# Seven products instead of eight for two token blocks of the second weight chunk, in an attention + experts + MLP kernel

## The chip, the core and the metric

One core of a Trainium2 chip runs the kernel. The metric is the device time of one execution in microseconds (us); the median of several executions counts. PE is the matrix engine, DVE the vector engine, ACT the scalar engine, POOL the GpSimd engine, SP the engine whose queue issues the loads.

## The reference

Sliding-window attention with sink tokens gives x (1536 tokens by 512). A mixture of eight experts follows, its gate balanced by eight rounds of row and column scaling, and then a two-layer MLP:

```python
P = np.exp(x @ w_gate - max)
for _ in range(8):
    P /= P.sum(1) + 1e-09;  P /= P.sum(0) + 1e-09;  P *= N / E
for e in range(8):
    out += P[:, e:e + 1] * (np.maximum(x @ w1[e], 0) @ w2[e])      # F = 1024
g = np.maximum(out @ w_in, 0) ** 2                                 # 2048 wide
return g @ w_out
```

Everything is float32.

## The kernel before, in words

**Chunks and blocks.** The weights are worked through in 20 chunks `c`, each 512 columns of a first matrix and the 512 matching rows of a second; 16 belong to the experts, 4 to the MLP. Chunk 0 runs as filler inside the attention (`phase_a`, its last groups at the start of `phase_b`), chunks 1 to 19 in `phase_b`. The tokens are three blocks `t` of 512. A float32 operand is held as a high and a low part, and one product of two operands is three matmuls. A split (`pair_split`, L480) writes the high part on ACT and then the low part on POOL.

**First product.** `plain(c, t, f)` makes 128 columns `f` of one block with 12 matmuls into one PSUM bank. From chunk 2 on `fast(c, half, 0)` (L793) makes two column groups of the blocks 0 and 1 together, as a two-by-two block product with seven multiplications instead of eight. Its seven steps are p1, p6, p5, p2, p7, p3, p4, of six matmuls each, each with an evacuation e1 to e4, e6 and so on behind it. It needs four sums of parts of x (`T1` to `T4`, made by `sums(0)` on DVE and split; T1 overwrites the part B12 of x) and four sums of weight parts (`unit_sums` on POOL, then split by `units(.., 3, ..)`). The third block has sums of its own (`sums(1)`). Step p1 fills a bank, e1 has ACT copy it to the scratch tile `x0` as `s`, and p2 goes on adding into the same bank, so p2 waits for that copy:

```python
def e1():
    v["s"] = self.scratch2("xs" if q else "x0", w)
    nc.scalar.activation(out=v["s"], in_=v["a"], func=AF.Copy)
...
def p2():
    mul("a", "A12", "B21")
```

The scratch tiles `x0`, `x1`, `x2` and `u` have one buffer each; who writes one waits until everything that read its last content is done. `sums` and the steps of `fast` share them.

**Second product.** `second(c, t)` (L899) is four groups of 12 matmuls; DVE adds each to `acc`.

**Order.** Every engine takes its instructions in the order in which the program issues them. `phase_b` builds a list `seq` of groups for a chunk and a `plan` of further steps behind each group; the position of a group in `seq` is called its position here. In chunk 1 the first run is a plain group and the three left groups of chunk 0. Then all three blocks go through `plain` (blocks 1, 0, then 2) with the second products between. `part_w2` splits the second matrix, `sums(0)` is made at positions 0 to 12 for chunk 2, `sums(1)` at positions 15 to 21, the weight sums of chunk 2 at positions 7 to 10.

**The gate** (`gate`, L946) is a generator with 14 steps: three logit steps of eight matmuls, the maximum, and eight rounds. In each round DVE makes the column sums `cs`, PE adds them over the partitions by one small matmul, and DVE scales P. One step is issued behind each group whose number is in `GATE_AT`. The weight `wgz` of the gate and the matrix `ones` are made at the start of `phase_b`. P is first needed in the second product of chunk 2.

**Loads.** `load_list` orders the 512 KB loads of the weights into three raw buffers; a load is issued when the one three places before it is used up.

Of the kernel before, what the change touches and what calls it, by code (L numbers as in the profile page):

```python
# [39 lines left out]
CONV_AT = (0, 1, 2, 3, 8, 9, 10, 11, 12, 13, 14, 15)  # L40
GATE_AT = (0, 1, 2, 3, 5, 7, 9, 11, 13, 16, 19, 22, 25, 30)
W2_AT = (2, 5, 8, 11)
# [6 lines left out]
class Kernel:  # L49
# [30 lines left out]
    def masks_begin(self):  # L80
# [19 lines left out]
        self.ident = c.tile([128, 128], F32, name="ident")  # L100
        make_identity(nc, self.ident)
        a = self.att
        self.junk = a.tile([128, 1], F32, name="junk")
# [332 lines left out]
    def load_list(self, c0):  # L436

        loads, k = [(c0, which, half) for which in range(2) for half in range(2)], 0
        for c in range(c0, NC):
            wide = [(j, 2, 0) for j in range(k, min(k + CONV, 8 * NC2)) if c >= 2]  # L440
            k += len(wide)
            n = c + 1
            loads += wide[0:1]
            if n < NC:
                if self.is_fast(n):
                    loads += [(n, 3, 0), (n, 3, 1)]
                loads += wide[1:2] + [(n, 0, 0)] + wide[2:3] + [(n, 0, 1), (n, 1, 0), (n, 1, 1)]
            else:
                assert len(wide) < 2
        return loads  # L450
# [219 lines left out]

    def sums(self, q):

        nc = self.nc
        T = [
            self.tp.tile([128, 3, 2, NB >> q], F32R, tag=f"T{q}{t}", name=f"T{q}{t}")
            for t in "hl"
        ]
        self.T[q] = T

# [9 lines left out]
        def put(name, kc, x):  # L689
            hi, lo = self.operand(name, q)  # L690
            self.pair_split(hi[:, kc], lo[:, kc], x)

        for kc in range(2):
            x = tt("x0", f32("B22", 0, kc), f32("B12", 0, kc), ALU.subtract)
# [347 lines left out]
    def run(self):  # L1042
# [18 lines left out]
        if True:  # L1061
            with tc.manual_schedule():
                first = ExitStack()
                self.wp = self.pool(first, "wp0")
                self.hp0 = self.pool(first, "hp0")
                with ExitStack() as actx:
                    self.wraw = self.pool(actx, "wraw0")
# [125 lines left out]
    def phase_a(self, gen):  # L1193
# [17 lines left out]
        for n in (HP - 1, HP):  # L1211
            self.att_load_qk(n)
        fill = self.filler(gen)
        at = next(fill)
        for u in range(U + 2):
# [57 lines left out]
            if u == 20:  # L1273
                self.general_flag()
        return fill

    def phase_b(self, c0, first, fill):
# [20 lines left out]
        self.next_loads()  # L1298
        self.wgz = self.xp_.tile([128, KD, 128], F32R, tag="x0", name="wgz")
        wgr = self.xp_.tile([128, KD, E], F32, tag="x2", name="wgr")  # L1300
        nc.gpsimd.memset(self.wgz.bitcast(F32), 0.0)
        self.ones = self.xp_.tile([128, 128], F32, tag="x1", name="ones")
        nc.gpsimd.memset(self.ones, 1.0)
        nc.sync.dma_start(out=wgr, in_=self.wg)
        todo = [partial(self.units, c0, half, 0, k) for half in range(2) for k in range(2)]
        for _ in fill:
# [7 lines left out]
        hz = self.wgz[:, :, 0:E]  # L1314
        nc.scalar.activation(out=hz, in_=wgr, func=AF.Copy)
        nc.vector.tensor_tensor(
            out=self.wgz[:, :, E : 2 * E], in0=wgr, in1=hz.bitcast(F32), op=ALU.subtract
        )
        gate = self.gate()
        groups = itertools.count()  # L1320

        def run(seq, plan):

            for k, g in enumerate(seq):
                g()
                for step in plan.get(k, ()):
                    step()
                if next(groups) in GATE_AT:
                    next(gate, None)
# [5 lines left out]
        for c in range(c0, NC):  # L1335
# [8 lines left out]
            if not low:  # L1344
                run([self.plain(c, 1, 0), *rest], {})
                low = first.close() or True
                self.w2p = self.pool(left, "w2" + n)
                self.tp = self.pool(left, "T" + n)
                self.cp, self.T = self.pool(left, "c" + n), {}
                seq = [self.plain(c, t, f) for t in (1, 0) for f in range(KD)][1:]  # L1350
# [10 lines left out]
            if self.is_fast(c):  # L1361
                (a, b, *e), (f, g, *i) = (self.fast(c, half, 1) for half in range(2))
# [13 lines left out]
            if c == NC1 - 1:  # L1376
# [3 lines left out]
                )  # L1380
                wide = lambda k: m + k if k < 8 else m + 2 * k - 8
            else:
                seq += self.second(c, 0) + self.second(c, 2)
                wide = lambda k: m + k
            if c in (FAST - 1, FAST2 - 1):
                t = self.sums(0)
                for k in range(13):
                    put(k if c < FAST else min(2 * k, k + 5), next, t, None)
# [111 lines left out]
```

## Time and profile before

| | |
|---|---|
| median of 3 runs | 1379.15 us (1378.8 to 1379.48) |
| profiled execution | 1379.64 us, of which the span from first to last instruction is 1377.8 us |
| busy in the span | PE 1363.2, DVE 955.4, POOL 501.3, ACT 453.1 us |
| granted clock of PE | 0.999 of full speed |
| attention ends on PE / chunk 1 starts / chunk 2 starts | 150.87 / 163.67 / 247.35 us |

The kernel is one chain of matmuls: PE is busy 99% of the span. The times of the last row are read from the start of the span. A bar on PE in the trace is longer than the distance to the next, since matmuls overlap; costs are taken from start to start.

### The profile page before, as it was taken

How to read it: one execution, taken by the hardware profiler on the slowest of the kernel's cores; microseconds unless marked ns; L12 is line 12 of the kernel's file. 1: busy time of each engine (PE TensorE's matmuls, PEld its weight loads, DVE VectorE, ACT ScalarE, POOL GpSimd, SP SyncE). 2: the span in 40 equal slices, each digit the busy share in tenths (PEclk: the TensorE clock that was granted, in tenths of full speed). 3: DMA queues.
4: the chain of work that ended last, by engine and by line, in shares of the span. 5: the costliest groups of instructions: out<-in, count | busy, mean ns of one | idle time of the engine just before them, and what ended most of it. 6: DMA issues, size and time to landing. Idle time of an engine off the chain costs nothing.

```text
span 1377.8 us, 18905 instructions
## 1 busy us (share of the span) xinstructions
PE 1363.2 (99%) x7105; PEld 1141.7 (83%) x7105; DVE 955.4 (69%) x1884; ACT 453.1 (33%) x1007; POOL 501.3 (36%) x442
## 2 busy tenths in 40 slices
PE   8999999999999999999999999999999999999998
PEld 5677888888888888888888888888888888888887
DVE  8777369887777777777777768765454568866564
ACT  6776322322232222222232222222232243433331
POOL 4322136524343434424343434423343036543210
PEclk9999999999999999999999999999999999999999
DMA  5222200132313232232313232230102010111101
GB/s 203 81 90 73 78 31 31 62 94 73 124 54 109 79 96 85 92 107 67 118 54 122 70 95 82 92 107 32 61 32 77 16 62 16 62 55 54 46 24 72
DMA packets 61147, 102.53 MB, mean 74 GB/s; under 512 B 3957, under 2 KB 43253, under 8 KB 60789
## 3 DMA queue, kind: packets, MB, share of 16 engines
q1 hardware_dynamic: 61040, 101.22, 23.2%
q8 instruction: 58, 0.95, 0.3%
q14 instruction: 45, 0.36, 0.1%
q10 hardware_dynamic: 4, 0.00, 0.0%
HBM read 89.67 MB, written 11.53 MB: 73 GB/s over the span
## 4 chain that ended last, share of the span: by engine, by line
PE 79%; DVE 1%; ACT 0%; issue 0%; DVEq 0%; ACTq 0%
PE mm L913 42%; PE mm L762 36%; PE mm L930 0%; ACT tx L733 0%; DVE acc L653 0%; DVE tx L734 0%; ACT hh L745 0%; DVE tx L822 0%; DVE hl L746 0%; DVE acc L649 0%; DVE mm L734 0%; DVE raw L578 0%; ACT tx L836 0%; DVE tu L822 0%; DVE raw L565 0%
## 5 line engine op out<-in xcount | busy, mean ns | idle before, releaser
L913 PE MATMUL mm<-w2h,hh 128*128 128x512 f32 (+1 forms) x916 | 357.0, 390 | 0.0
L913 PE MATMUL mm<-w2l,hh 128*128 128x512 f32 (+1 forms) x916 | 355.9, 388 | 0.0
L913 PE MATMUL mm<-w2h,hl 128*128 128x512 f32 (+1 forms) x916 | 355.6, 388 | 0.0
L482 POOL TENSOR_TENSOR w2l<-raw,w2h 128x512 fp32r<-128x512 f32 x76 | 118.5, 1559 | 365.7 <-ACT w2h L481 363.7
L653 DVE SCALAR_TENSOR_TENSOR acc<-mm,P,acc 128x512 f32<-128x512 f32 x168 | 125.7, 748 | 135.6 <-PE mm L913 134.4
L913 PEld LDWEIGHTS mm<-w2h,hl 128*128 128x128 f32 x916 | 172.0, 188 | 35.8
L913 PEld LDWEIGHTS mm<-w2h,hh 128*128 128x128 f32 x916 | 172.1, 188 | 34.6
L913 PEld LDWEIGHTS mm<-w2l,hh 128*128 128x128 f32 x916 | 172.1, 188 | 34.3
L525 POOL TENSOR_TENSOR raw<-raw 128x256 f32<-128x256 f32 x136 | 125.1, 923 | 7.9
L482 POOL TENSOR_TENSOR s0l<-raw,s0h 128x512 fp32r<-128x512 f32 (+1 forms) x36 | 45.5, 1264 | 198.6 <-ACT s0h L481 198.6
L730 ACT ACTIVATE hh<-tx 128x512 fp32r<-128x512 f32 (+1 forms) x112 | 58.8, 525 | 130.0 <-DVE tx L822 129.5
L822 DVE TENSOR_TENSOR tx<-mm,tu 128x512 f32<-128x512 f32 (+1 forms) x136 | 75.6, 556 | 20.9 <-PE mm L762 16.6
L822 DVE TENSOR_TENSOR tx<-mm,tx 128x512 f32<-128x512 f32 (+1 forms) x68 | 37.9, 557 | 57.8 <-PE mm L762 56.5
L740 DVE SCALAR_TENSOR_TENSOR hl<-tx,hh 128x512 fp32r<-128x512 f32 (+1 forms) x112 | 70.1, 626 | 9.7 <-ACT hh L730 9.6
L836 ACT ACTIVATE tx<-mm 128x512 f32<-128x512 f32 x34 | 20.3, 598 | 154.9 <-PE mm L762 153.0
L646 DVE TENSOR_TENSOR acc<-mm,acc 128x512 f32<-128x512 f32 (+1 forms) x49 | 33.2, 677 | 48.2 <-PE mm L913 47.9
L730 ACT ACTIVATE hh<-mm 128x512 fp32r<-128x512 f32 (+1 forms) x68 | 34.0, 501 | 99.2 <-PE mm L762 99.2
L836 ACT ACTIVATE txs<-mm 128x256 f32<-128x256 f32 x34 | 13.0, 381 | 151.3 <-PE mm L762 151.3
L482 POOL TENSOR_TENSOR a0l<-raw,a0h 128x512 fp32r<-128x512 f32 (+1 forms) x38 | 43.0, 1148 | 51.5 <-ACT a0h L481 47.5
L762 PE MATMUL mm<-xl,a1h 128*128 128x512 f32 (+1 forms) x172 | 60.3, 350 | 0.2 <-ACT tx L836 0.2
L762 PE MATMUL mm<-xl,a0h 128*128 128x512 f32 (+1 forms) x172 | 59.8, 348 | 0.0
L762 PE MATMUL mm<-xh,a0h 128*128 128x512 f32 (+1 forms) x172 | 59.8, 347 | 0.0
(262 smaller groups left out, 3149.5 us busy)
## 6 DMA issues: line engine op xcount, KB each, us to landing
raw<-w SPq DMA_DIRECT2D x110, 512.0 KB, 3.7
raw<-win SPq DMA_DIRECT2D x16, 512.0 KB, 4.0
w<-m SPq DMA_DIRECT2D x32, 256.0 KB, 4.6
raw<-wout SPq DMA_DIRECT2D x16, 512.0 KB, 4.0
raw<-qkv SPq DMA_DIRECT2D x8, 624.0 KB, 5.0
raw<-qkv SPq DMA_DIRECT2D x7, 464.0 KB, 3.9
out<-acc SPq DMA_DIRECT2D x11, 256.0 KB, 2.0
wraw<-w SPq DMA_DIRECT2D x2, 1024.0 KB, 6.7
```

The lines of the kernel that those rows point to most:

```text
L482: self.nc.gpsimd.tensor_tensor(out=lo, in0=src, in1=hi.bitcast(F32), op=ALU.subtract)
L525: self.nc.gpsimd.tensor_tensor(out=o, in0=x, in1=y, op=op)
L646: nc.vector.tensor_tensor(out=a, in0=ps, in1=a, op=ALU.add)
L653: nc.vector.scalar_tensor_tensor(out=a, in0=ps, scalar=self.P[:, ti, e : e + 1], in1=a, op0=ALU.mult, op1=ALU.add)
L730: nc.scalar.activation(out=hh, in_=src, func=AF.Relu)
L740: nc.vector.scalar_tensor_tensor(out=hl, in0=src, scalar=0.0, in1=hh.bitcast(F32), op0=ALU.max, op1=ALU.subtract,)
L762: self.nc.tensor.matmul(out=ps, lhsT=w[:, kc], rhs=x[:, kc], start=start and k == 0, stop=(k == n - 1), skip_group_check=True,)
L822: nc.vector.tensor_tensor(out=v[name], in0=v[a], in1=v[b], op=ALU.add)
L836: nc.scalar.activation(out=v["s"], in_=v["a"], func=AF.Copy)
L913: self.nc.tensor.matmul(out=ps[:, d], lhsT=x[:, f, s], rhs=w[:, f, d], start=(n == 0), stop=(n == 11),)
```

## The change

Chunk 1 is reordered. The third block goes first and stays plain, its second product follows, then blocks 0 and 1 go through `fast` together, and their second products end the chunk. So the first product of chunk 1 has 84 matmuls in two blocks where it had 96.

For that the sums of x must be there earlier. T1 is made in the end of the attention's filler, behind the three logit steps of the gate (T1 overwrites a part of x that they read). T2, T3 and T4 are made at positions 3 to 8 of chunk 1, under the second product of the third block and the first steps of `fast`. The weight sums of chunk 1 are new work: two more loads of 512 KB, eight POOL additions and four splits. The gate's weight is loaded and split inside the attention (units 20 and 25), `ones` is made at the kernel's start. Ten steps of the gate are left for the groups numbered 12 to 41.

```diff
-GATE_AT = (0, 1, 2, 3, 5, 7, 9, 11, 13, 16, 19, 22, 25, 30)
+GATE_AT = (
+    (0, 1, 2, 3, 5, 7, 9, 11, 13, 16, 19, 22, 25, 30),
+    (12, 15, 18, 21, 24, 27, 30, 33, 37, 41),
+)
...
+        self.ones = c.tile([128, 128], F32, name="ones")
+        nc.gpsimd.memset(self.ones, 1.0)
...
+        if c0:
+            loads[2:2] = [(c0, 3, 0)]
+            loads.append((c0, 3, 1))
...
+    def sums(self, q, t1_first=False):
...
+        if t1_first:
+            for kc in range(2):
+                x = tt("x0", f32("B12", 0, kc), f32("B11", 0, kc), ALU.subtract)
+                tt(x, x, f32("B12", 1, kc), ALU.add)
+                tt(x, x, f32("B11", 1, kc), ALU.subtract)
+                put("T1", kc, x)
+                yield
+            self.T_tiles(q)
+            t2 = []
+            for kc in range(2):
+                x = tt(("u", "x1")[kc], f32("B22", 0, kc), f32("B12", 0, kc), ALU.subtract)
+                tt(x, x, f32("B22", 1, kc), ALU.add)
+                tt(x, x, f32("B12", 1, kc), ALU.subtract)
+                put("T2", kc, x)
+                t2.append(x)
+                yield
+            for kc in range(2):
+                x = tt("x0", t2[kc], f32("B11", 0, kc), ALU.subtract)
+                tt(x, x, f32("B11", 1, kc), ALU.subtract)
+                put("T3", kc, x)
+                yield
+            for kc in range(2):
+                x = tt("x2", f32("B21", 0, kc), t2[kc], ALU.subtract)
+                tt(x, x, f32("B21", 1, kc), ALU.add)
+                put("T4", kc, x)
+                yield
+            return
...
+            if u in (20, 25):
+                gw.pop(0)()
...
+    def gate_weights(self, pool, tags):
...
+        def load():
+            nc.gpsimd.memset(self.wgz.bitcast(F32), 0.0)
+            nc.sync.dma_start(out=wgr, in_=self.wg)
+
+        def split():
+            nc.scalar.activation(out=hz, in_=wgr, func=AF.Copy)
+            nc.gpsimd.tensor_tensor(
+                out=self.wgz[:, :, E : 2 * E], in0=wgr, in1=hz.bitcast(F32), op=ALU.subtract
+            )
...
+            early = [partial(next, gate)] * 3 + [partial(next, t0)] * 2
+            early += [partial(self.unit_sums, c0, 0, k) for k in range(2)]
+            early.append(partial(next, gate))
+        for at in fill:
             if self.done:
                 self.evac()
                 if todo:
                     todo.pop(0)()
+                if early and (at == NT - QW or len(early) > 5):
+                    early.pop(0)()
         self.evac()
-        for step in todo:
+        for step in todo + early:
             step()
...
-                run([self.plain(c, 1, 0), *rest], {})
+                run([self.plain(c, 1 + c0, 0), *rest], {})
...
+            mixed = c == c0 == 1
             for k in range(4):
-                put(W2_AT[k] if self.is_fast(c) else k, self.part_w2, c, k)
+                if mixed:
+                    self.part_w2(c, k)
...
+            if mixed:
+                m += 18
+                put(2, self.finish)
+                seq += self.second(c, 2) + self.fast(c, 0, 0) + self.fast(c, 1, 0)
+                seq += self.second(c, 1)
+                for k in range(2):
+                    put(2 + 2 * k, self.units, c, 0, 3, k)
+                    put(6 + k, self.unit_sums, c, 1, k)
+                    put(8 + k, self.units, c, 1, 3, k)
...
+            elif mixed:
+                seq += self.second(c, 0)
+                wide = lambda k: m - 8 + k
...
+                t = t0 if mixed else self.sums(0)
+                for k in range(7 if mixed else 13):
+                    put(k + 3 if mixed else min(2 * k, k + 5) if c >= FAST else k, next, t, None)
                 t = self.sums(1)
                 for k in range(13):
-                    put(m + 8 + k // 2, next, t, None)
+                    put(m + (k // 2 if mixed else 8 + k // 2), next, t, None)
```

In the new chunk 1 the positions are: 0 to 2 plain groups of block 2, 3 to 6 its second product, 7 to 13 the steps p1, p6, p5, p2, p7, p3, p4 of the first half, 14 to 20 those of the second half, 21 to 24 the second product of block 1, 25 to 28 that of block 0. Group number is position plus 4.

## Rows read from the trace of the kernel before

**Rows 1.** The page: the span, and the busy time of each engine.
```profile
span 1377.8 us, 18905 instructions
...
PE 1363.2 (99%) x7105; PEld 1141.7 (83%) x7105; DVE 955.4 (69%) x1884; ACT 453.1 (33%) x1007; POOL 501.3 (36%) x442
```

**Rows 2.** Busy time by stretch: from and to, length, then each engine, clock, DMA.
```profile
150.87:163.67 12.80, 12.80 (x69) 12.02 (x68) 4.21 (x7) 4.35 (x10) 6.16 (x10) 1.00 0.53 169
163.67:181.70 18.03, 18.03 (x86) 14.14 (x85) 2.28 (x5) 2.97 (x6) 0.00 (x0) 1.00 0.08 28
...
204.50:226.90 22.40, 22.18 (x102) 18.11 (x101) 21.05 (x36) 6.26 (x11) 15.27 (x15) 1.00 0.00 1
226.90:247.35 20.45, 20.45 (x95) 16.99 (x93) 18.62 (x39) 4.80 (x11) 11.02 (x12) 1.00 0.24 78
```

**Rows 3.** PE in order of time, chunk 2: first matmuls of p1, p6 and p2.
```profile
247.35 0.39 PE L762 MATMUL mm<-xl,a0h 128*128 128x512 f32 x1
...
248.71 0.39 PE L762 MATMUL mm<-T0l,s0h 128*128 128x512 f32 x1
...
251.43 0.39 PE L762 MATMUL mm<-xl,a0h 128*128 128x512 f32 x1
```

**Rows 4.** PE in order of time: the two waits in chunks 1 and 2.
```profile
210.04 0.39 PE L913 MATMUL mm<-w2h,hl 128*128 128x512 f32 x1
210.64 0.39 PE L1001 MATMUL mm<-cs,ones 128*128 128x8 f32 x2 [0.21 <-DVE cs L995]
...
280.99 0.28 PE L762 MATMUL mm<-xh,a0l 128*128 128x256 f32 x1
281.86 0.39 PE L762 MATMUL mm<-xl,s0h 128*128 128x256 f32 x1 [0.59 <-DVE tx L822]
```

**Rows 5.** DVE in order of time: sums of x, evacuations, one round of the gate.
```profile
186.03 1.79 DVE L683 TENSOR_TENSOR tx<-tx,tu 128x512 f32<-128x512 f32 x1
...
190.46 1.78 DVE L683 TENSOR_TENSOR tu<-xl 128x512 f32<-128x512 f32 x1
192.17 0.68 DVE L740 SCALAR_TENSOR_TENSOR hl<-mm,hh 128x512 fp32r<-128x512 f32 x1
...
198.44 0.68 DVE L683 TENSOR_TENSOR tu<-xl 128x512 f32<-128x512 f32 x1
199.04 0.68 DVE L740 SCALAR_TENSOR_TENSOR hl<-mm,hh 128x512 fp32r<-128x512 f32 x1
...
204.78 0.69 DVE L646 TENSOR_TENSOR acc<-mm,acc 128x512 f32<-128x512 f32 x1
...
230.17 0.20 DVE L1005 RECIPROCAL cs<-mm 128x8 f32<-128x8 f32 x1
...
231.67 0.35 DVE L995 TENSOR_REDUCE cs<-P 128x8 f32<-128x104 f32 x1
```

**Rows 6.** POOL in order of time: attention, start of the weights, low parts, weight sums.
```profile
72.16 2.32 POOL L205 TENSOR_TENSOR qkl<-raw,qkh 128x640 fp32r<-128x640 f32 x2 [9.03 <-ACT qkh L204]
...
151.06 0.53 POOL L1301 MEMSET wgz<- 128x512 f32 x1 [20.92 <-PE xp L388]
151.53 0.20 POOL L1303 MEMSET ones<- 128x128 f32 x1
...
185.99 1.29 POOL L482 TENSOR_TENSOR w2l<-raw,w2h 128x512 fp32r<-128x512 f32 x1 [23.89 <-ACT w2h L481]
...
191.65 1.73 POOL L482 TENSOR_TENSOR w2l<-raw,w2h 128x512 fp32r<-128x512 f32 x1
...
216.50 1.57 POOL L525 TENSOR_TENSOR raw<-raw 128x256 f32<-128x256 f32 x2
```

**Rows 7.** ACT in order of time, chunk 2: the copy `s` and a split.
```profile
249.34 0.58 ACT L836 ACTIVATE tx<-mm 128x512 f32<-128x512 f32 x1
249.82 0.62 ACT L481 ACTIVATE w2h<-raw 128x512 fp32r<-128x512 f32 x1
```

**Rows 8.** The page, DMA issues: count, size, median us to landing.
```profile
raw<-w SPq DMA_DIRECT2D x110, 512.0 KB, 3.7
```

More of the change, by code (lines that the diff above doesn't have):

```diff
@@ L669, in operand, with T_tiles @@
         return tuple(x[:, k : k + 2, o : o + w] for x in (self.xh, self.xl))
-    def sums(self, q):
-        nc = self.nc
-        T = [
+    def T_tiles(self, q):
+        self.T[q] = [
             self.tp.tile([128, 3, 2, NB >> q], F32R, tag=f"T{q}{t}", name=f"T{q}{t}")
@@ L677, in sums @@
         ]
-        self.T[q] = T
+    def sums(self, q, t1_first=False):
+        nc = self.nc
         def tt(o, a, b, op):
@@ L691, in put @@
             self.pair_split(hi[:, kc], lo[:, kc], x)
+        if t1_first:
[25 more added lines that the diff above has]
+            return
+        self.T_tiles(q)
         for kc in range(2):
@@ L1065, in run @@
                 self.hp0 = self.pool(first, "hp0")
+                self.gw = self.pool(first, "gw0")
                 with ExitStack() as actx:
@@ L1212, in phase_a @@
             self.att_load_qk(n)
+        gw = list(self.gate_weights(self.gw, ("wgz", "wgr")))
         fill = self.filler(gen)
@@ L1274, in phase_a @@
                 self.general_flag()
-        return fill
+            if u in (20, 25):
+                gw.pop(0)()
+        return fill
+    def gate_weights(self, pool, tags):
+        nc = self.nc
+        self.wgz = pool.tile([128, KD, 128], F32R, tag=tags[0], name="wgz")
+        wgr = pool.tile([128, KD, E], F32, tag=tags[1], name="wgr")
+        hz = self.wgz[:, :, 0:E]
+        def load():
[6 more added lines that the diff above has]
+            )
+        return load, split
     def phase_b(self, c0, first, fill):
@@ L1298, in phase_b @@
         self.next_loads()
[L1299 to L1304, printed above, removed]
-        todo = [partial(self.units, c0, half, 0, k) for half in range(2) for k in range(2)]
-        for _ in fill:
+        if not c0:
+            for step in self.gate_weights(self.xp_, ("x0", "x2")):
+                step()
+        todo = [partial(self.units, c0, half, 0, k) for half in range(2) for k in range(2)]
+        gate, early = self.gate(), []
+        if c0:
+            t0 = self.sums(0, True)
+            early = [partial(next, gate)] * 3 + [partial(next, t0)] * 2
+            early += [partial(self.unit_sums, c0, 0, k) for k in range(2)]
+            early.append(partial(next, gate))
+        for at in fill:
             if self.done:
@@ L1310, in phase_b @@
                     todo.pop(0)()
+                if early and (at == NT - QW or len(early) > 5):
+                    early.pop(0)()
         self.evac()
-        for step in todo:
+        for step in todo + early:
             step()
[L1314 to L1319, printed above, removed]
         groups = itertools.count()
@@ L1327, in run @@
                     step()
-                if next(groups) in GATE_AT:
+                if next(groups) in GATE_AT[c0]:
                     next(gate, None)
@@ L1349, in phase_b @@
                 self.cp, self.T = self.pool(left, "c" + n), {}
-                seq = [self.plain(c, t, f) for t in (1, 0) for f in range(KD)][1:]
+                seq = [self.plain(c, t, f) for t in ((2,) if c0 else (1, 0)) for f in range(KD)]
+                seq = seq[1:]
             elif self.is_fast(c):
@@ L1354, in phase_b @@
                 seq = [self.plain(c, t, f) for t in (1, 0) for f in range(KD)]
+            mixed = c == c0 == 1
             for k in range(4):
-                put(W2_AT[k] if self.is_fast(c) else k, self.part_w2, c, k)
+                if mixed:
+                    self.part_w2(c, k)
+                else:
+                    put(W2_AT[k] if self.is_fast(c) else k, self.part_w2, c, k)
             if c == NC1:
@@ L1360, in phase_b @@
             m = len(seq)
[L1361 removed]
+            if mixed:
[7 more added lines that the diff above has]
+                    put(8 + k, self.units, c, 1, 3, k)
+            elif self.is_fast(c):
                 (a, b, *e), (f, g, *i) = (self.fast(c, half, 1) for half in range(2))
@@ L1385, in phase_b @@
             if c in (FAST - 1, FAST2 - 1):
-                t = self.sums(0)
-                for k in range(13):
-                    put(k if c < FAST else min(2 * k, k + 5), next, t, None)
+                t = t0 if mixed else self.sums(0)
+                for k in range(7 if mixed else 13):
+                    put(k + 3 if mixed else min(2 * k, k + 5) if c >= FAST else k, next, t, None)
                 t = self.sums(1)
                 for k in range(13):
-                    put(m + 8 + k // 2, next, t, None)
+                    put(m + (k // 2 if mixed else 8 + k // 2), next, t, None)
             if c + 1 < NC:
```

## The prediction

> **What bounds the kernel now.** I read the page first. PE is busy 1363.2 of 1377.8 us [rows 1], so a microsecond of matmul taken out is a microsecond of time, as long as nobody makes PE wait. The stretches around the change come next [rows 2]: from the attention's end to chunk 2 PE has no hole but one, and its clock is granted in full. But DVE is busy 21.05 of 22.40 us in the middle of chunk 1 and 18.62 of 20.45 at its end, while in the 18 us before position 0 it has 2.28 us of work and POOL none. So the new work goes into a stage where DVE is nearly full, on a path where PE is full. The order of PE in time gives the price of a step: p1 to p6 is 1.36 us for six matmuls, 0.2267 us each [rows 3]. The two places where PE does wait are both for a late DVE: 0.37 us beyond a matmul's 0.227 at a column sum of the gate in chunk 1, and 0.75 beyond 0.12 in the third block of chunk 2 [rows 4].
>
> **What it removes.** 96 first-product matmuls become 84: 12 x 0.2267 = 2.72 us. With the sums of x rearranged, the wait at 210 us has no reason to stay: 0.37 us. Together 3.1 us if all else hides. The wait in chunk 2 has its causes in chunk 2 and stays.
>
> **What it moves at no cost.** `ones` and `wgz` are 0.20 and 0.53 us of POOL [rows 6]; in the attention POOL stands idle for 9 us between two pieces of 2.3 us, so they hide there, and so does the small load of the gate's weight, which leaves the loads' queue between two attention loads. Uncovered, they would cost 0.7 us. The three logit steps and the maximum are the same PE work in another place, so position 0 still begins at 181.7. T1 has six differences on DVE where DVE was idle; through ACT it delays the evacuation of the last filler group to about 175.3, and the group that needs it reaches that part at about 175.5. I take 0, between 0 and 1 us. The new load for the second half can be issued when POOL has read its buffer, about 199, and lands 3.7 us later [rows 8], before POOL comes to it at 205; nothing.
>
> **The shared port.** A difference of two SBUF tiles takes DVE 0.68 us alone, but 1.79 us when it starts at 186.03, just after POOL's low part of 1.29 us started at 185.99 [rows 5, 6]. It ends 0.54 us after POOL does: it waited for POOL to end. And it holds POOL up in turn: POOL's piece at 191.65 takes 1.73 instead of 1.29, with DVE's difference of 190.46 ending 0.5 us into it. An operation with one input in PSUM is not touched: 0.68 at 192.17, in the middle of that piece [rows 5]. So these DVE operations and all POOL pieces run one after the other. With that order kept, the sum below comes to +10.5 us; with the same operations free of each other it would be +0.2. The Trainium skill has a rule for it that speaks against this change (GPSIMD Engine Reference, Key points): GpSimd shares its SBUF interfaces with VectorE and contends with instructions that have two SBUF inputs. By that rule the larger of the two sums holds, and the trace agrees with it (1.79 against 0.68 us).
>
> **The first wait, at p2 of the first half.** I laid the queues of DVE, ACT and POOL out in the order in which they are issued, at 0.6 us from start to start for a 512-column DVE operation, 0.5 (0.6 to its end) for ACT [rows 7], 1.25 for a low part and 0.73 for a weight sum on POOL [rows 5, 6]. The same count for the order of before gives PE waits at 210.8 and 281.9 of 0.5 and 0.8 us (the rows have 0.37 and 0.75) and starts chunk 2 at 247.3, as the trace does; that is why I trust it here. PE: three plain groups from 181.7 to 189.9, four second-product groups of 2.72 to 200.7, p1, p6, the gate's maximum (0.36) and p5, and p2 is due at 205.1. DVE behind it:
> - 192.8 first add, then T2's first half, three differences: 195.2. ACT, and POOL's low part 195.9 to 197.2.
> - 195.5 second add, then T2's second half, 196.1 to 200.2: held by that low part and by the split of the weight sums behind it (197.2 to 199.0).
> - 200.2 third add; T3's first half 200.8 to 203.2, one of two differences held by T2's low part; fourth add to 203.8; POOL has T3's low part until 205.2.
> - T3's second half wants `x0`, free at 205.25. POOL has two weight sums from 205.2, which alternate with its two differences: 207.9. ACT 208.5, POOL's low part, one T4 difference in its way, to 210.2.
> - Now `x0` is free for the copy `s` of e1: ACT 210.3 to 210.9. PE's p2 starts at 210.95.
>
> That is 5.8 us. In chunk 2 of before, the same copy starts at 249.34 [rows 7], 2.1 us ahead of p2 at 251.43 [rows 3], because no sum of x holds `x0`. The bounds: without port conflicts 0.9 us, with each piece 0.05 us longer 6.1. I take 5.8, since the conflicts are in the rows.
>
> **The later waits.** Behind `s`, DVE does `u` (211.6) and T4's second half, which wants `x2` (free at 213.0, when POOL has read T4's first half) and meets one more low part: 215.5. The gate's maximum is queued behind it on DVE, 215.9. PE has its next gate step behind p7, due at 213.7: 2.2 us (0 to 2.4). p3, p4 and, in the second half, p2 and p4 add into banks that a late ACT or DVE has to read first: 0.1, 0.3, 0.5, 0.5, together 1.4 (0 to 2). DVE then has the ten additions and eight low parts of `hl` of the two halves, and two rounds of the gate at 1.8 us each (230.17 to the end of 231.67 plus 0.35 [rows 5]), with eight weight sums of chunk 2 on POOL's side of the port; the column sums behind position 17 come at 227.0, when PE has stood since 225.7: 1.4 (0 to 1.5). By the same count DVE enters the last eight groups 4 to 5 us behind. They hold `sums(1)`, as the end of chunk 1 did before, where DVE had 1.83 us to spare in 20.45 [rows 2]; so some 3 us are left when PE, behind the first step of chunk 2, comes to the column sums: I take 2.8 (0 to 3.6).
>
> **Sum.** -2.72 - 0.37 + 5.8 + 2.2 + 1.4 + 1.4 + 2.8 = +10.5 us against the profiled execution's 1379.64, which is its span of 1377.8 and 1.84 us around it: 1390.1. That execution lies 0.49 above the median, so 1389.6. Chunk 2 starts 7 us later than before, the rest comes in chunk 2; from chunk 3 on nothing differs.
>
> One cost no row prices: in these stretches PE never stands longer than 0.6 us [rows 4], and its clock stays at its full level [rows 2]. The Trainium skill (TensorE: Matmul & The Clock Gate, Part 1) says that an idle PE falls to half its clock until it has been busy again; no run here shows that for a wait like this one. I add nothing: a slower PE would also let DVE catch up, so that part of the later waits would go.
>
> **The rivals.**
> - *All hides, the kernel gets faster.* PE is the busiest engine and loses 12 matmuls. It needs DVE to hand over `s` by 205.1. For it: T1 lies in an idle stretch and the rest mostly under second products, which ask little of DVE. Against it: from 192.8 on, the ten differences up to T3 are 6.0 us and POOL's pieces in between 7.7 (five splits and two weight sums), on one port; even with the adds under them that is 206.5, and the copy 0.6 more, 2 us over. Time: 1379.15 - 3.1 = 1376.1. The Trainium skill's general advice (Perfetto Trace Analysis, Identifying the Most-Contended Engine) is to work on the engine with the highest occupancy first, with the weight loads as measure for PE; PE's are at 83% and the highest after its matmuls. By that rule this case holds.
> - *Nothing gained, nothing lost.* The differences and POOL's pieces happen to miss each other. Then the waits are 0.9 at `s`, 1.0 at the maximum and 1.4 in small ones: 1379.4. The pieces are triggered by the differences, so they can't miss each other often.
> - *Half the loss.* The first two waits come, then DVE has caught up, since a waiting PE hands it nothing: -3.1 + 5.8 + 2.2 = +4.9, 1384.1. It decides at the second half: if DVE's `u` there is not late.
> - *More.* The load for the second half lands 3 us later than counted, or T1 holds the first groups up by its full 1 us, and everything behind it shifts: 1391 to 1394.
>
> **How the numbers follow.** The forecast's case has 0.60, half the loss 0.20, more 0.07, nothing 0.08, faster 0.05. The range from 1383.5 to 1393.5 takes in the forecast, half the loss and the near part of more, and leaves out the two cases at 1379.4 and below: about 0.83. This kernel's measurements can tell 0.2%, 2.76 us: faster (below 1376.4) 0.05, same 0.08, slower (above 1381.9) 0.87.
>
> **What would show it.** In the trace of the changed kernel PE stands for some 6 us ahead of the fourth step of the first half, released by ACT's copy of the bank to `tx`, and that copy by POOL's low part of T3. T2's and T3's differences take 1.2 to 1.8 us where POOL works. A second wait of about 2 us ahead of the matmul with `nm`, and 1 to 3 us ahead of two column sums. Chunk 2's first matmul comes at about 254 instead of 247.35. I would be wrong if the copy is there by 205, which means that DVE passed POOL faster than in the rows; or if the T1 part in the filler holds up the first groups, which I priced at nothing.

## The result, and the profile after

The changed kernel takes 1390.74 us (median of 4 runs, 1388.78 to 1391.54), the kernel before 1379.32 beside it: a ratio of 1.0081, 95% interval 1.0063 to 1.0098. It is slower, by 11.4 us where 10.5 were forecast. The profiled spans differ by 11.0 us (1388.8 and 1377.8).

The page of the changed kernel, span and busy times:
```profile
span 1388.8 us, 18919 instructions
...
PE 1365.5 (98%) x7093; PEld 1141.3 (82%) x7093; DVE 962.1 (69%) x1893; ACT 456.7 (33%) x1013; POOL 513.1 (37%) x455
```
PE has 12 instructions fewer than in [rows 1] and is busy 2.3 us longer all the same, mostly since it ran some of them at half clock (3.3 us by the count below). The waits of PE by line (who waits, on whom; us in total, times, longest), changed kernel:
```profile
PE mm L799 <- ACT tx L873: 5.5, 1, 5.5
...
PE mm L1038 <- DVE cs L1032: 2.6, 2, 1.9
PE mm L799 <- DVE tx L859: 1.2, 3, 0.6
...
PE mm L1020 <- DVE nm L1017: 0.4, 1, 0.4
```
Line 799 is the products' matmul (762 before), 873 the copy `s`, 1038 the gate's column sum (1001 before), 1020 its maximum. The first row is the forecast's first wait. Here it is in the timeline of all engines (start, length, engine, line, out<-in, then the idle time before it and what ended it):
```profile
204.50 1.29 POOL L490 TENSOR_TENSOR T0l<-tx,T0h 128x512 fp32r<-128x512 f32 x1 [1.29 <-ACT T0h L489]
205.41 0.40 PE L799 MATMUL mm<-xh,s0l 128*128 128x512 f32 x1
205.74 1.85 POOL L533 TENSOR_TENSOR raw<-raw 128x256 f32<-128x256 f32 x2
205.82 1.20 DVE L692 TENSOR_TENSOR tx<-tx,xh 128x512 f32<-128x512 f32 x1 [1.46 <-POOL T0l L490]
207.05 1.09 DVE L692 TENSOR_TENSOR tx<-tx,xl 128x512 f32<-128x512 f32 x1
...
208.88 1.71 POOL L490 TENSOR_TENSOR T0l<-tx,T0h 128x512 fp32r<-128x512 f32 x1 [1.29 <-ACT T0h L489]
210.62 0.60 ACT L873 ACTIVATE tx<-mm 128x512 f32<-128x512 f32 x1 [1.82 <-POOL T0l L490]
211.27 0.80 PE L799 MATMUL mm<-xl,a0h 128*128 128x512 f32 x1 [5.46 <-ACT tx L873]
211.87 0.63 PE L799 MATMUL mm<-xh,a0h 128*128 128x512 f32 x1
...
214.82 0.40 PE L799 MATMUL mm<-T0h,s0l 128*128 128x512 f32 x1
215.05 0.39 PE L799 MATMUL mm<-T0l,s0h 128*128 128x512 f32 x1
```
Read it from the end. PE stops after 205.41 and starts again at 211.27, when ACT's copy is there; the copy waited for GpSimd's low part of T3's second half (208.88), which has to leave `x0`; that half's differences (205.82, 207.05) began when the low part of the first half had left the same `x0`, and took 1.20 and 1.09 us instead of 0.68 beside the weight sums of POOL. Behind the wait eight matmuls stand 0.43 us apart and not 0.2267.

Busy time by stretch, changed kernel (from and to, length, PE, PEld, DVE, ACT, POOL, granted clock, DMA):
```profile
181.00:200.70 19.70, 19.70 (x88) 16.33 (x87) 10.41 (x13) 5.66 (x10) 9.63 (x7) 1.00 0.16 54
200.70:219.60 18.90, 12.74 (x47) 9.30 (x46) 12.62 (x18) 6.21 (x11) 13.26 (x12) 0.82 0.09 28
219.60:235.00 15.40, 14.14 (x63) 10.81 (x62) 14.61 (x31) 5.47 (x10) 8.30 (x10) 1.00 0.11 35
...
256.00:280.00 24.00, 22.14 (x94) 18.05 (x93) 18.83 (x40) 9.40 (x17) 9.57 (x9) 0.93 0.14 45
```
The granted clock is at 0.82 in the stretch of the first wait and at 0.93 in chunk 2's beginning; before, it was at its full level all through chunk 1 [rows 2]. Note also that DVE is half idle ahead of the wait (10.41 of 19.70 us). The other waits that count, PE in order of time:
```profile
215.52 0.40 PE L799 MATMUL mm<-T0h,s0l 128*128 128x512 f32 x1
216.27 0.38 PE L1020 MATMUL mm<-nm,ones 1*128 1x1 f32 x2 [0.35 <-DVE nm L1017]
...
227.14 0.39 PE L1038 MATMUL mm<-cs,ones 128*128 128x8 f32 x2 [0.75 <-DVE cs L1032]
...
254.76 0.39 PE L799 MATMUL mm<-xl,a0h 128*128 128x512 f32 x1
...
258.15 0.39 PE L1038 MATMUL mm<-cs,ones 128*128 128x8 f32 x2 [1.86 <-DVE cs L1032]
...
260.05 0.63 PE L799 MATMUL mm<-T0h,s0l 128*128 128x512 f32 x1
260.47 0.63 PE L799 MATMUL mm<-xl,s0h 128*128 128x512 f32 x1
```
VectorE at the same place, from the first addition of the last eight groups (the group ends on PE at 235.24) to the column sum of 258 us:
```profile
236.59 0.68 DVE L654 TENSOR_TENSOR acc<-mm,acc 128x512 f32<-128x512 f32 x1
...
255.38 0.98 DVE L692 TENSOR_TENSOR tx<-tx,xl 128x256 f32<-128x256 f32 x1
256.28 0.20 DVE L1042 RECIPROCAL cs<-mm 128x8 f32<-128x8 f32 x1
...
257.76 0.34 DVE L1032 TENSOR_REDUCE cs<-P 128x8 f32<-128x104 f32 x1
```
The last sums (255.38) stand ahead of the gate's round (256.28 to 258.10).

Taken from start to start, over what the same matmuls cost at full clock, the excesses are 5.63 at p2, 1.71 at half clock behind it, 0.72 at the maximum (0.43 and 0.29), 1.13 in three small waits (0.29, 0.29, 0.55), 0.91 and 2.02 at the two column sums and 1.55 at half clock behind the last: 13.67. Less the 3.09 saved, that is 10.6 of the 11.0 us; the other 0.4 aren't assigned. Small steps of about 0.1 us belong to them: counted from the attention's end, position 0 comes after 31.39 us (182.37) instead of 30.83 (181.70).

### The profile page after: what moved, and what is told of

Its sections match the earlier page's. It is cut to its first block, busy times and chain, and to the rows that moved or that the text cites. A ratio compares the mean times of both kernels' runs of the same rounds, so it can differ in the third digit from the quotient of the medians.

```text
span 1388.8 us, 18919 instructions
## 1 busy us (share of the span) xinstructions
PE 1365.5 (98%) x7093; PEld 1141.3 (82%) x7093; DVE 962.1 (69%) x1893; ACT 456.7 (33%) x1013; POOL 513.1 (37%) x455
## 4 chain that ended last, share of the span: by engine, by line
PE 78%; DVE 0%; issue 0%; DVEq 0%
PE mm L950 42%; PE mm L799 36%; PE mm L967 0%; DVE acc L661 0%; DVE acc L657 0%; DVE raw L586 0%; DVE tx L859 0%; DVE tu L859 0%; DVE raw L573 0%; DVE acc L654 0%; DVE raw L582 0%; DVE raw L578 0%; DVEq L661 0%; DVE m L590 0%; DVEq L859 0%
## 5 line engine op out<-in xcount | busy, mean ns | idle before, releaser
L533 POOL TENSOR_TENSOR raw<-raw 128x256 f32<-128x256 f32 x144 | 130.7, 911 | 11.4 <-DVE m L565 1.9
L490 POOL TENSOR_TENSOR s0l<-raw,s0h 128x512 fp32r<-128x512 f32 (+1 forms) x38 | 48.9, 1288 | 205.9 <-ACT s0h L489 205.9
L777 DVE SCALAR_TENSOR_TENSOR hl<-tx,hh 128x512 fp32r<-128x512 f32 (+1 forms) x116 | 73.2, 631 | 10.0 <-ACT hh L767 9.7
L490 POOL TENSOR_TENSOR a1l<-raw,a1h 128x512 fp32r<-128x512 f32 (+1 forms) x38 | 39.9, 1069 | 59.6 <-ACT a1h L489 59.6
L767 ACT ACTIVATE hh<-mm 128x512 fp32r<-128x512 f32 (+1 forms) x62 | 30.5, 492 | 90.5 <-PE mm L799 90.5
L777 DVE SCALAR_TENSOR_TENSOR hl<-tu,hh 128x512 fp32r<-128x512 f32 (+1 forms) x58 | 58.8, 1014 | 1.5
```

The source lines that it names most:

```text
L490: self.nc.gpsimd.tensor_tensor(out=lo, in0=src, in1=hi.bitcast(F32), op=ALU.subtract)
L533: self.nc.gpsimd.tensor_tensor(out=o, in0=x, in1=y, op=op)
L767: nc.scalar.activation(out=hh, in_=src, func=AF.Relu)
L777: nc.vector.scalar_tensor_tensor(out=hl, in0=src, scalar=0.0, in1=hh.bitcast(F32), op0=ALU.max, op1=ALU.subtract,)
```

## The experiments

The theory: VectorE and GpSimd hand T2 to T4 to each other through one port and two scratch tiles, so the chain runs late, and every wait of PE is that lateness seen at another place. The rivals: the one tile `x0` is what delays the copy; the half clock is a cost of its own; spacing the gate costs; or the stage has no room on VectorE in any order. Ratios are to runs of the kernel before on the same chip: 1379.73 us for the first four runs, 1379.65 for the last sums later, the gate alone and the first of the other places, 1379.31 for the gate as before and the first run with shared low parts, 1379.90 for the second order and the last run.

**The tile.** T3's second half in `x2` instead of `x0`.
```diff
-                x = tt("x0", t2[kc], f32("B11", 0, kc), ALU.subtract)
+                x = tt(("x0", "x2")[kc], t2[kc], f32("B11", 0, kc), ALU.subtract)
```


> T3's second half is made in scratch x2 instead of x0, so that x0 is free for the copy s some 5 us earlier. Port theory (DVE and POOL share one port, and the sums of x come too late for it): the copy comes earlier, the wait ahead of p2 falls from 5.6 to about 2.3 us, but DVE is as late as before and T4 now waits for x2; the gate's maximum waits about 6 us instead of 0.4. Time 1390 to 1392, as with the change. Buffer theory (only the single buffer x0 makes PE wait): the wait of 5.6 us and the slow clock behind it (1.7 us) go, and nothing comes in their place: 1383 to 1384.

1390.11 us, ratio 1.0079 (1.0063 to 1.0096): no gain. PE in order of time, this run:
```profile
204.43 0.39 PE L799 MATMUL mm<-xh,s0l 128*128 128x512 f32 x1
206.87 0.50 PE L799 MATMUL mm<-xl,a0h 128*128 128x512 f32 x1 [2.06 <-ACT tx L873]
...
215.60 0.58 PE L1020 MATMUL mm<-nm,ones 1*128 1x1 f32 x2 [5.71 <-DVE nm L1017]
...
257.47 0.39 PE L1038 MATMUL mm<-cs,ones 128*128 128x8 f32 x2 [1.87 <-DVE cs L1032]
```
This trace runs 0.98 us ahead of the changed kernel's (PE's last matmul before p2 is at 204.43, there at 205.41). Counted from that matmul p2 comes 3.4 us earlier (2.44 and 5.86 us), and the maximum, which stands behind T4 on VectorE, as late as ever (11.17 and 10.86). The tile only names the wait, as the port theory expected.

**The sums earlier.** T2 to T4 at positions 0 to 5 instead of 3 to 8.
```diff
-                    put(k + 3 if mixed else min(2 * k, k + 5) if c >= FAST else k, next, t, None)
+                    put(k if mixed or c < FAST else min(2 * k, k + 5), next, t, None)
```


> T2 to T4 at positions 0 to 5 instead of 3 to 8, 8.2 us earlier, all else as in the change. Port theory: DVE and POOL have the same work in the same order, only sooner; the wait ahead of p2 falls to 0.2 us, there is no slow clock behind it, the column sums still wait about 1 and 2 us in the second half and 3 us (with 1.5 us of slow clock) at the start of chunk 2: 1383 to 1385. Gate theory (the new places of the gate's steps are what costs): the waits of the gate's steps keep the time near 1390.

1385.76 us, 1.0044 (1.0027 to 1.0061): 5 us of the loss gone, the time 0.8 above the expected range. p2 waits 0.37. One wait that no theory had: the second products stand for 2.03 us at 193.33, for a relu that is queued on ACT behind T2's high part, which is late itself because the low parts of w2 hold VectorE's differences.
```profile
193.33 0.50 PE L950 MATMUL mm<-w2h,hh 128*128 128x512 f32 x1 [1.87 <-ACT hh L767]
193.67 0.40 PE L950 MATMUL mm<-w2l,hh 128*128 128x512 f32 x1
...
253.32 0.39 PE L1038 MATMUL mm<-cs,ones 128*128 128x8 f32 x2 [1.86 <-DVE cs L1032]
```
The last row is the column sum in chunk 2. It waits 1.86 us as in the changed kernel, though T2 to T4 are early.

**GpSimd out of it.** The low parts of T2 to T4 are written by ACT as a second copy of the sum, so the remainders of the split are left out.
```diff
+            if t1_first and name != "T1":
+                nc.scalar.activation(out=hi[:, kc], in_=x, func=AF.Copy)
+                nc.scalar.activation(out=lo[:, kc], in_=x, func=AF.Copy)
+                return
```


> The low parts of T2 to T4 are written by ACT as a plain copy instead of by POOL as a difference; the true low parts are left out. DVE's work is the same to the instruction, POOL has six pieces less on the port, ACT has six more. Port theory: the differences of T2 to T4 fall to about 0.7 us, no wait ahead of p2, about 1 us at the gate's maximum, 1.4 and 3 us at column sums: 1383 to 1385. Rival (DVE's own amount of work is too much, whatever POOL does): the differences may get shorter, but PE still waits 4 us or more ahead of p2: 1388 to 1391.

1385.31 us, 1.0037 (1.0023 to 1.0051), 0.3 above the expected range. The wait at p2 shrinks to 1.16 us; PE stands 0.81 us for the maximum where it stood 0.35, and no half clock follows (granted clock 1.00 from 200 to 222 us). T3's second half on VectorE, this run:
```profile
203.57 0.74 DVE L692 TENSOR_TENSOR tx<-tx,xh 128x512 f32<-128x512 f32 x1 [0.62 <-ACT T0l L702]
204.35 0.69 DVE L692 TENSOR_TENSOR tx<-tx,xl 128x512 f32<-128x512 f32 x1
```
With VectorE's own work unchanged, six GpSimd operations less, and six copies more on ACT, are worth 5.4 us. The time alone doesn't tell the port from the chain that GpSimd's parts are a link of. The lengths show that the port has a part: these two took 1.20 and 1.09 us above, and all fourteen differences of T2 to T4 take 12.1 us in sum here and 14.6 in the changed kernel. How the 5.4 us divide between the two isn't shown.

**The clock.** 24 matmuls without use, into a spare bank, ahead of p2 in the first half: they fill the wait.
```diff
+            if c == 1 and half == 0:
+                spare = self.mmtile()[:, 0:w]
+                for _ in range(4):
+                    self.products(
+                        spare, [(self.weight(c, half, 0), self.operand("B11", q))], start=True
+                    )
```


> 24 matmuls that nobody needs are put ahead of p2 of the first half of chunk 1: 5.4 us of work in the place of 5.5 us of waiting, so that PE never stands long there. The granted clock should stay full from 211 to 215 us. Port theory: the 1.7 us of slow clock were time in which DVE caught up, so they come back as a wait of about 2 us at the gate's maximum: 1390 to 1391, as with the change. Clock theory (the slow matmuls are a cost of their own): 1.7 us faster, 1388.5 to 1389.2.

1391.23 us, 1.0085 (1.0068 to 1.0102), 0.2 above the expected range. The matmuls behind p2 now run at full clock, and the time that this gives back is waited for at the next step:
```profile
215.74 0.38 PE L1026 MATMUL mm<-nm,ones 1*128 1x1 f32 x2 [2.00 <-DVE nm L1023]
```
2.00 us against 0.35: the maximum is there when VectorE has it, at whichever clock PE comes to it. Half clock behind p2 costs nothing of its own. The run does not take the half clock out of the stage: a stretch of it follows behind this wait instead (217.13 to 220.54 us, 1.6 lost), and the waits behind it, 1.49 us in the changed kernel up to its column sum at 227.14, are 0.13 here. So this stretch, too, is paid for by waits, all but 0.2 us.

**The last sums later.** Chunk 2's third-block sums one product later, behind the column sum on VectorE.
```diff
-                    put(m + (k // 2 if mixed else 8 + k // 2), next, t, None)
+                    put(m + (1 + k // 2 if mixed else 8 + k // 2), next, t, None)
```


> One number of the schedule: the last sums of the third block (chunk 2's first operands) are made one product later in its second half, so that VectorE comes to the first column sum of chunk 2's gate before them. VectorE's-queue theory: the column sum's wait of 1.86 us at 258 us and the stretch at half clock behind it (about 1.5 us) both go, and TensorE's other waits stay: the 5.5 us at 205 to 211 us, and those at 216 to 231 us. That is 1390.7 less 3.3: 1387 to 1388 us. Rival, that the wait only moves on (VectorE is as full behind it, so that chunk 2's first products then wait for the sums that are late): 1389.5 to 1391 us, with a wait of about 2 us at 254 to 264 us under another name. If the half clock comes of itself at that place, without a wait ahead of it, a stretch of about 1.5 us is left: 1388.5 to 1389.5.

1387.45 us, 1.0060 (1.0044 to 1.0075). The wait at 258 us and the stretch at half clock behind it are gone (clock 1.00 from 250 to 280 us); a wait of 0.72 at 262 us is new. So that wait was one of order alone, and the expected 1387 to 1388 holds. The 5.47 us at p2 stay.

**The gate alone.** The order of products of before, with the gate's weights and first four steps in the attention's end and its other ten three groups apart. Against the changed kernel:
```diff
-    (12, 15, 18, 21, 24, 27, 30, 33, 37, 41),
+    (8, 11, 14, 17, 20, 23, 26, 29, 33, 37),
...
-            mixed = c == c0 == 1
+            mixed = False
```


> The kernel before with only the gate's part of the change: its weights come in the attention's end, four of its steps run there, and the other ten stand three groups apart; the products keep the order of before. Two waits of TensorE were there before, 0.37 us at 211 us and 0.59 us at 282 us. VectorE's-queue theory: spacing the gate is nearly free by itself, since the order of before leaves VectorE room: within 0.5 us of before, 1378.9 to 1379.8 us, with no new wait over 0.5 us at 195 to 235 us. Rival, that the gate's spread steps (its maximum and the step behind it, its column sums) are what costs: 2 to 5 us more, 1381 to 1384 us, with waits of the gate's column sums and its maximum in TensorE's row.

1383.21 us, 1.0025 (1.0016 to 1.0034): my expectation of 1378.9 to 1379.8 missed, and the time lies in the rival's range. Up to 250 us there is no wait, as expected; then a column sum is 2.31 us late. PE, and below it the gate's round ahead of that sum on VectorE, beside GpSimd:
```profile
253.27 0.60 PE L1035 MATMUL mm<-cs,ones 128*128 128x8 f32 x2 [2.31 <-DVE cs L1029]
253.72 0.77 PE L796 MATMUL mm<-xl,a0h 128*128 128x512 f32 x1
254.29 0.63 PE L796 MATMUL mm<-xh,a0h 128*128 128x512 f32 x1
```
```profile
249.52 1.99 POOL L487 TENSOR_TENSOR a1l<-raw,a1h 128x512 fp32r<-128x512 f32 x2
249.64 1.29 DVE L1040 SCALAR_TENSOR_TENSOR P<-P,cs 128x96 f32<-128x96 f32 x1
...
251.47 1.25 POOL L487 TENSOR_TENSOR w2l<-raw,w2h 128x512 fp32r<-128x512 f32 x1
251.53 1.32 DVE L1026 TENSOR_TENSOR P<-P,rs 128x96 f32<-128x96 f32 x1
```
It is a collision of the gate's step with chunk 2's work, as at 258 us in the changed kernel, but another one. There the last sums stand ahead of the round; here they are done at 248.3, and two operations of the round take 1.29 and 1.32 us beside GpSimd's parts, where the same two take 0.26 and 0.36 in the changed kernel's round at 256.51 and 257.36. That is the port, without any of T2 to T4. Of the ten runs of this kernel five have a mean clock of 0.999 or 1.0 and take 1381.6 to 1382.4 us, five 0.997 or 0.998 and 1384.0 to 1385.3, the profiled one among them: by that clock the half-clock stretch came in half of the executions, and the two groups lie some 2.3 us apart.

**The gate as before.** The new order of products with the ten steps where they were.
```diff
-    (12, 15, 18, 21, 24, 27, 30, 33, 37, 41),
+    (5, 7, 9, 11, 13, 16, 19, 22, 25, 30),
```


> The changed kernel with the gate's ten spread steps at the places of before (5, 7, 9, 11, 13, 16, 19, 22, 25, 30) instead of 12 to 41: the new order of products without the spacing. VectorE's-queue theory: the first products that waited 5.5 us no longer do so alone; the stall is cut up over the gate's column sums (about 3.3, 3.8, 2 and 1 us between 204 and 226 us in the laid-out queues), and the wait at 258 us is gone, 8.6 us over before in sum and 1.5 us for each stretch at half clock that a wait brings: 1389 to 1393 us. Rival, that the spacing is what costs: within 3 us of before, 1377 to 1382.

1389.18 us, 1.0070 (1.0054 to 1.0085). The waits by line, this run:
```profile
PE mm L1038 <- DVE cs L1032: 7.6, 3, 3.2
...
PE mm L799 <- DVE tx L859: 2.1, 3, 1.3
```
The long wait is cut into pieces of 3.24, 2.86 and 1.50 us at column sums, as expected, and the sum stays. In this order of products the spacing changes the total by 1.6 us only. That does not make it free: in the order of before it cost 3.6 us, in the run with the gate alone.

**Other places for the same work.** T2 to T4, the gate's steps, the unit sums and the last sums put elsewhere, from laying out the queues of VectorE, GpSimd and ACT with the rows' durations.
```diff
-    (12, 15, 18, 21, 24, 27, 30, 33, 37, 41),
+    (12, 15, 20, 22, 24, 27, 30, 35, 39, 44),
...
-                    put(6 + k, self.unit_sums, c, 1, k)
+                    put(5 + k, self.unit_sums, c, 1, k)
...
-                    put(k + 3 if mixed else min(2 * k, k + 5) if c >= FAST else k, next, t, None)
+                    put((0, 2, 2, 4, 4, 7, 8)[k] if mixed else min(2 * k, k + 5) if c >= FAST else k, next, t, None)
...
-                    put(m + (k // 2 if mixed else 8 + k // 2), next, t, None)
+                    put(m + (1 + k // 2 if mixed else 8 + k // 2), next, t, None)
```


> The changed kernel with four numbers of its schedule changed, in order to keep VectorE's and GpSimd's queues from meeting: the seven pieces of T2 to T4 at products 0, 2, 2, 4, 4, 7, 8 of the third block's second products instead of 3 to 9, the gate's spread steps at 12, 15, 20, 22, 24, 27, 30, 35, 39, 44, the second half's unit sums one product earlier, and the last sums of the third block one product later. VectorE's-queue theory: the queues laid out in their order of issue with the durations of the rows give 1.4 us less than before, with about 2 us of waits left in chunk 1's second half: 1377 to 1379.5 us, if no wait is long enough to bring the half clock, and 1379 to 1381 with one such stretch. Rival, that the change's work has no room on VectorE in that stage in any order (it is 92 to 94 per cent busy there): the waits only move, and it stays at 1383 us or more. Rival, that all the waits go: 1376 to 1377 us.

1379.28 us, 0.9998 (0.9989 to 1.0007), inside the expected range: the whole loss is gone, and the gain is not there yet. The longest wait left is 0.96 us, at a column sum. A second such order, with nothing but places changed, against the changed kernel:

```diff
-    (12, 15, 18, 21, 24, 27, 30, 33, 37, 41),
+    (15, 18, 25, 27, 31, 34, 36, 38, 42, 44),
...
-                    put(6 + k, self.unit_sums, c, 1, k)
-                    put(8 + k, self.units, c, 1, 3, k)
+                    put(8 + k, self.unit_sums, c, 1, k)
+                    put(11 + k, self.units, c, 1, 3, k)
...
-                    put(k + 3 if mixed else min(2 * k, k + 5) if c >= FAST else k, next, t, None)
+                    put((1, 2, 2, 4, 4, 7, 7)[k] if mixed else min(2 * k, k + 5) if c >= FAST else k, next, t, None)
...
-                    put(m + (k // 2 if mixed else 8 + k // 2), next, t, None)
+                    put(m + ((0, 0, 1, 1, 1, 1, 1, 3, 3, 5, 5, 5, 5)[k] if mixed else 8 + k // 2), next, t, None)
```


> The changed kernel's operations, all of them on their own engines, with only their places in the queues changed: T2 to T4 at products 1, 2, 2, 4, 4, 7, 7, the gate's steps at 15, 18, 25, 27, 31, 34, 36, 38, 42, 44, the second half's unit sums and their splits two and three products later, and the last sums of the third block grouped by twos to fives. VectorE's-queue theory: what the changed kernel lost it lost to the order alone, and this order loses almost none: the laid-out queues give 2.7 us under before with no wait over 0.55 us, 1376.5 to 1378 us. If the layout misses one wait of 1 to 2.5 us, 1378 to 1380.5. Rival, that the work has no room in that stage whatever the order: 1379.5 us or more, with waits that sum up to over 2.5 us between 195 and 265 us.

1378.88 us, 0.9993 (0.9984 to 1.0002), with the longest wait at 0.62 us; 1376.5 to 1378 was expected. Then the low parts of the first halves of T3 and T4 by VectorE, in the first of these orders and in a third:
```diff
-            self.pair_split(hi[:, kc], lo[:, kc], x)
+            if t1_first and kc == 0 and name in ("T3", "T4"):
+                nc.scalar.activation(out=hi[:, kc], in_=x, func=AF.Copy)
+                tt(lo[:, kc], x, hi[:, kc].bitcast(F32), ALU.subtract)
+            else:
+                self.pair_split(hi[:, kc], lo[:, kc], x)
```


> The schedule of the run with four numbers changed, and besides the low parts of the first halves of T3 and T4 are made by VectorE (one tensor_tensor of 0.68 us each) instead of GpSimd (1.3 to 1.8 us each, and VectorE's operation behind it waits for it). Port theory: taking two GpSimd operations out of that stage gives VectorE back more than the two operations cost it; the queues laid out with the rows' durations give 1 us less than that run, with the waits at 208 to 211 us gone and the column sum's of about 1 us left: 1377.5 to 1379 us. Rival, that VectorE's busy time is what counts (two operations more on an engine at 92 to 94 per cent): 1379.5 to 1381 us, with the waits at 208 to 211 us longer than 0.75 us in sum.

The third order, against the changed kernel (the edit of the low parts above is in it too):
```diff
-    (12, 15, 18, 21, 24, 27, 30, 33, 37, 41),
+    (13, 17, 24, 27, 31, 33, 35, 37, 42, 44),
...
-                    put(6 + k, self.unit_sums, c, 1, k)
+                    put(5 + k, self.unit_sums, c, 1, k)
...
-                    put(k + 3 if mixed else min(2 * k, k + 5) if c >= FAST else k, next, t, None)
+                    put((1, 2, 2, 4, 4, 7, 8)[k] if mixed else min(2 * k, k + 5) if c >= FAST else k, next, t, None)
...
-                    put(m + (k // 2 if mixed else 8 + k // 2), next, t, None)
+                    put(m + ((1, 1, 3, 3, 3, 3, 3, 3, 3, 6, 7, 7, 7)[k] if mixed else 8 + k // 2), next, t, None)
```


> The run with two low parts on VectorE, in another order: T2 to T4 at 1, 2, 2, 4, 4, 7, 8, the gate at 13, 17, 24, 27, 31, 33, 35, 37, 42, 44, the last sums grouped. VectorE's-queue theory: the laid-out queues give 2.8 us under before, with one wait of about 0.75 us at a column sum near 248 us: 1376.5 to 1378 us. If one piece comes a step late there, 2.6 us of wait at that column sum and half clock behind it: 1379 to 1381 us. Rival, that VectorE's busy time is what counts and no order helps: 1379.5 us or more.

The first takes 1378.14 us, 0.9992 (0.9983 to 1.0001), the second 1377.69 us, 0.9987 (0.9978 to 0.9996): the second is the one version whose interval lies below the kernel before. Both lie in the range expected first. Two operations more on VectorE and two fewer on GpSimd make it no slower, as the port theory has it. The waits of the products' and the gate's matmuls in the second are one row, and its stretches show where the work went:
```profile
PE mm L1042 <- DVE cs L1036: 1.2, 2, 0.8
```
```profile
181.50:200.70 19.20, 19.20 (x86) 15.92 (x85) 13.69 (x17) 6.88 (x12) 11.82 (x8) 1.00 0.17 55
200.70:219.60 18.90, 18.90 (x85) 15.03 (x84) 15.63 (x28) 7.46 (x13) 16.53 (x16) 1.00 0.16 55
219.60:235.00 15.40, 15.40 (x71) 12.68 (x70) 14.51 (x28) 4.92 (x9) 7.61 (x7) 1.00 0.16 49
```
VectorE does 13.69 us in the stretch ahead of p2 where the changed kernel did 10.41, and PE never stands from 181.5 to 235 us. The rival without room falls.

## Why the prediction was right

The forecast was 1389.6, its mechanism the shared port, and the first wait came where and as it was laid out: 5.63 us against 5.8, released by the copy, and that by T3's low part. Chunk 2 starts at 254.76, where 254 was written; the sum's own terms up to there (all but the last 2.8) would have put it at 255.1.

- **The port.** Differences of T3 took 1.20 and 1.09 us beside GpSimd instead of 0.68; with GpSimd's parts of T2 to T4 away they took 0.74 and 0.69, and 5.4 us came back. The Trainium skill's rule (GPSIMD Engine Reference, Key points), that the two contend when VectorE reads two SBUF inputs, agrees with that.
- **The maximum and the clock: two terms whose sizes changed places.** The step "gate's maximum, 2.2" measured 0.72, the clock that I "add nothing" for 1.71; 2.43 together against 2.2. The reason given holds for the first stretch: filled with useless work, the wait moved to the maximum and the total stayed. It does not hold for the second: behind the column sum at 258 us no wait followed that could have given it back, and 1.55 us were lost. That term was mis-sized.
- **The column sums and the small waits.** 1.4, 1.4 and 2.8 measured 0.91, 1.13 and 2.02. With the 1.55 the seven come to 13.67 against 13.6; that the sum fits so well is luck, two errors against each other.
- **The reason for the 2.8 does not hold.** It was to be what is left of a VectorE that enters the last eight groups 4 to 5 us late. In the trace VectorE comes to the first addition of these groups at 236.59, 1.4 us behind the group's end at 235.24. And the wait is the same, 1.86 and 1.89 us, in the runs with the sums earlier and with GpSimd out of it, while it goes when the last sums stand one product later. So it is the gate's step meeting the last sums, which other places undo, and not lateness carried on from p2. The size was near by luck. (Two slips in the working change nothing: the difference of 190.46 ends 0.59 us, not 0.5, into POOL's piece, and 227.0 less 225.7 is 1.3, not 1.4.)
- **T1 in the attention's end at nothing, and the old wait at 210 us gone.** Right within the bound of 1 us: there is no long wait at the filler's last groups, though position 0 comes 0.56 us later, counted from the attention's end, and 0.26 of that come in the run with the gate alone, which has no T1 there. The column sum that waited at 210 us has moved with the gate, so its 0.37 went into the terms above.
- **The premise that the stage is nearly full on DVE** was read from the order of before [rows 2]. In the new order DVE is half idle ahead of p2; the work was late, not too much. So the loss belonged to the places chosen and not to the change, and the rival "all hides" described a kernel that other places come near to: some 2 of its 3.1 us by the last version, which also makes two low parts on VectorE.
- **The advice to work on the most contended engine first**, judged for PE by its weight loads (the Trainium skill, Perfetto Trace Analysis, Identifying the Most-Contended Engine), spoke for the case with 1376.1. PE is the bound, but taking 12 matmuls off it moved the end only where the helpers' chain had slack.

## What to carry to other kernels

When work comes off a full engine, lay out the helpers' queues in issue order, with the operations of VectorE and GpSimd that share a port one after the other; the engine's share over a stage does not tell whether a chain arrives in time. A wait that vanishes is only worth what the next wait behind it on the same queue leaves: freeing the tile, filling the hole and cutting the gate differently each left the total within 2 us. Look for idle time of the helper ahead of the stall; moving the chain there, with the gate's steps and the last sums moved too, gave all of it back.

## What the hardware showed unexpectedly

PE's granted clock fell behind some waits and not behind others of the same length. The column sum's wait at 258 us brought a stretch at the lower level (matmuls 0.43 us apart, which is about 1.2 GHz, instead of 0.2267 at 2.4) after 1.86 us in the changed kernel, and none after 1.87 us in the run with the tile freed (clock 1.00 from 250 to 280 us). In the run with the gate as before, waits of 3.24 and 2.86 us kept the full clock, and it fell behind the fourth of four within 18 us (0.79 from 222 to 230 us). The Trainium skill (TensorE: Matmul & The Clock Gate, Part 1) says that an idle PE falls to half its clock until it has been busy again; after 5.46 us it did, but these rows show that the length of the wait alone does not tell, and what does stays open here. It differs between executions of one kernel too: the run with the tile freed has two at a mean clock of 0.996 and 1388.6 and 1388.7 us, the profiled one among them, and two at 0.994 and 1391.5 and 1391.7; the gate alone has five and five.

The port cost a short operation as much as a long one: in the gate-alone run a VectorE operation of 96 columns, 0.26 us elsewhere, took 1.29 us beside GpSimd's low parts, and one of 0.36 us took 1.32.
